# Decode attention with a gated FFN on one core: loading the query weights first, and rearranging the output projection's feeders

## The chip, the core and the metric

The kernel runs on one core of a Trainium2 chip. The metric is the device time in microseconds (us), as the median of several executions. One execution was also recorded by the hardware profiler; its span, 198.8 us, is counted from the first instruction to the last and is a little shorter than the device time of the same execution (200.62 us).

## What is computed

Four decode tokens (B = 4) go through two branches that are mixed by a scalar gate per token. Cut to what matters:

```python
def _A_ref(x, k_cache, v_cache, wq, wo):          # B=4, D=512, Hq=32, Hkv=8, Dh=128
    W = 4096                                      # last 4096 of 16384 cached positions
    q = (x @ wq).reshape(B, 1, 32, 128)           # wq: 512 x 4096
    k = repeat(k_cache[:, :, Sk - W:, :], 4)      # 8 kv heads, each used by 4 query heads
    v = repeat(v_cache[:, :, Sk - W:, :], 4)
    p = softmax(q @ k.T * 128 ** -0.5)
    return (p @ v).reshape(B, 1, 4096) @ wo       # wo: 4096 x 512

def _B_ref(x, W_gate, W_up, W_down):              # 512 x 1792, 512 x 1792, 1792 x 512
    h = relu(x @ W_gate) * (x @ W_up)
    return h @ W_down

g = sigmoid((x * gate_w).sum(-1))
out = g * _A_ref(x, ...) + (1 - g) * _B_ref(x, ...)
```

All of it is bf16 in memory. The keys and values in the window are 4 x 8 x 4096 x 128 elements each, 33.5 MB each. With the weights, 81 MB are read from HBM.

## The kernel before

**Sets.** The attention work is cut into eight sets. Set s is token s % 4 with key-value heads 4*(s // 4) to 4*(s // 4) + 3, so each set reads 4 MB (4096 KB) of keys and 4 MB of values. The 128 partitions of a set hold 4 heads x 32 position blocks of 128 positions.

**Stages of one set.** In the code's names: `KT(s, f)`, four pieces f, turns a quarter of the keys with VectorE's block transpose (`EKT`, L510). `SC(s, f)` multiplies it on TensorE with the query block `qblk` and adds a mask (9 matmuls). `ESC` (L538) copies the scores from PSUM to SBUF and keeps their maxima. After the fourth piece, `MAX`, `SW` and `ESW` (L542 to L550) form one maximum per head. `EXP` (L617) is the softmax's exponential on ScalarE; `PT` (L554) turns the probabilities with a block transpose; `RS` sums the rows; `PV` multiplies the probabilities with the values (32 matmuls); `NORM` (L595) scales the result into `osb`, which has two buffers; `OQ` folds one set's rows of `osb` into the layout that the output projection wants (16 matmuls of 32 columns), and `EOQ` (L602) copies that into `oq`.

**Ends of the kernel.** Before the first set, `XT` turns x, `Z` makes the gate's sum, `Q` multiplies x with wq (32 matmuls), and `EQ`, `QT`, `EQT` spread the queries into `qblk`. After the last scores, `GU` multiplies x with W_gate and W_up (32 matmuls into two PSUM banks, four column groups of the array side by side; the columns of a group are picked with a stride of 14 elements so that the later turn comes out right), `RELU` (L610) and `H` (L562) make the hidden row, `HT` turns it with four TensorE transposes, `EHT` (L568) copies it to SBUF, and `FFN` multiplies it with W_down (28 matmuls) into PSUM bank 7. `T2` (L571) takes that result out of bank 7 and scales it by 1 - g. `WO(p)` then multiplies `oq` with wo in six pieces (64 matmuls) into the same bank 7, `FIN` (L575) adds the two branches, and two small stores write the output.

**Who decides the order.** Everything is written out by hand. `_order()` lists the stages; each engine runs its share of that list in that order, so a stage that waits on TensorE holds every later TensorE stage. `_dma_order()` lists the loads, and all of them are issued by one queue (SP, L247) in that order: a load that has to wait for its buffer holds every load behind it. `_slots()` gives the 4 MB loads four buffers in turn (wg and wu share one), and says what frees each: the fourth `KT` of a set frees its keys, `PV` its values, `Q` the query weights, `GU` the gate and up weights. Waits are put in by name: `WO(p)` waits for its piece of wo, for `T2` (since both results use bank 7) and for every `EOQ`.

The loads of wo in the order of their pieces are 8, 8, 8, 4, 2 and 2 of 32 blocks:

```python
WO_PIECES = ((0, 8), (8, 16), (16, 24), (24, 28), (28, 30), (30, 32))
```

Of the kernel before, what the change touches and what calls it, by code (L numbers as in the profile page):

```python
# [6 lines left out]
BF16 = mybir.dt.bfloat16  # L7
# [9 lines left out]
FF = 1792  # L17
# [78 lines left out]
def _alloc(nc, ctx):  # L96
    R = {}

    def sb(name, shape, dt):
        R[name] = ctx.enter_context(nc.sbuf_tensor(name, shape, dt))  # L100

    sb("slots", [128, NSLOT, 16384], BF16)
    sb("kt", [128, 4, 4096], BF16)
    sb("sc", [128, 2048], BF16)
    sb("pe", [128, 2048], BF16)
    sb("pT", [128, 2, 2048], BF16)
    sb("qblk", [128, NSET, 4, 144], BF16)
    sb("xsb", [4, 512], BF16)
    sb("xT", [128, 16], BF16)
    sb("hT", [128, 56], BF16)  # L110
    sb("gwT", [128, 4], BF16)
    sb("osb", [128, 2, 512], BF16)
# [24 lines left out]


def _order():
    o = [("XT",), ("Z",), ("KT", 0, 0), ("KT", 0, 1), ("KT", 0, 2), ("KT", 0, 3), ("Q",), ("QT",)]  # L140
    o += [("SC", 0, 0), ("SC", 0, 1), ("SC", 0, 2)]
    for s in range(1, NSET):
        o += [("KT", s, 0), ("SC", s - 1, 3)] + [("OQ", s - 2)] * (s > 1) + [("SW", s - 1), ("KT", s, 1), ("PT", s - 1)]
        o += [("SC", s, 0), ("KT", s, 2), ("SC", s, 1), ("RS", s - 1), ("KT", s, 3), ("SC", s, 2), ("PV", s - 1)]
    s = NSET - 1
    o += [("SC", s, 3), ("OQ", s - 1), ("SW", s), ("PT", s), ("RS", s), ("GU",), ("HT",), ("PV", s), ("OQ", s), ("FFN",)]
    return o + [("WO", p) for p in range(len(WO_PIECES))]


def _dma_order():  # L150
    o = [("k", 0), ("x",), ("gw",), ("wq",), ("k", 1), ("v", 0)]
    for s in range(2, NSET):
        o += [("k", s), ("v", s - 1)]
    return o + [("wg",), ("wu",), ("v", NSET - 1), ("wd",)] + [("wo", p) for p in range(len(WO_PIECES))]
# [23 lines left out]
def _program(nc, plan, R, aps):  # L178
# [4 lines left out]
    slots, kt, sc, pe, pT, qblk = R["slots"], R["kt"], R["sc"], R["pe"], R["pT"], R["qblk"]  # L183
    xsb, xT, gwT, osb, oq, hT = R["xsb"], R["xT"], R["gwT"], R["osb"], R["oq"], R["hT"]
    identb, identf, ones = R["identb"], R["identf"], R["ones"]
# [13 lines left out]
    Wo = slot("wo", 0).rearrange("p (i c) -> p i c", i=32)  # L199
    grelu, hrow = sc[:, 0:512], sc[:, 512:1024]  # L200

    trf, scf = {}, {}
    for it in order:
        k = it[0]
        if k == "QT":
            for n in range(2):
                for x in range(2):
                    trf[("QT", n, x)] = len(trf)
        elif k in ("XT", "SW", "RS", "OQ", "HT"):
# [100 lines left out]
    def tensor(t):  # L310
# [41 lines left out]
        def SC(s, f):  # L352
            key = ("SC", s, f)
            bk = banks[scb(key)]
            kv = kt[:, f, :].rearrange("p (t c h k e) -> p t c h k e", t=2, c=16, h=2, k=32)
            w = sc_free(key) + [("QB",), ("ML",), ("MR",), ("E", "KT", s, f)]
            for t in range(2):
# [25 lines left out]

        def OQ(s):
            key = ("OQ", s)
            r = 64 * (s // 4)
            for t in range(2):
                for cc in range(2):
                    for c in range(4):
                        x = 256 * t + 128 * cc + 32 * c  # L390
                        first, lastmm = (t, cc, c) == (0, 0, 0), (t, cc, c) == (1, 1, 3)
                        mm(banks[tr(key)][r:r + 64, 0:32], R["fold"][:, 2 * cc + t, c, :], osb[:, s % 2, x:x + 32], first,
                           lastmm, ev=key if lastmm else None, pos=(0, r),
                           waits=tr_free(key) + [("NORM", s), ("FOLD", 7)] if first else ())

        def gu_n(j):
            return 512 if j < 2 else 384

        def gu_cols(W, q, j):
            g = W[:, FF * q:FF * q + FF].rearrange("p (k i) -> p i k", i=14)  # L400
            return g[:, j:14:4, :]
# [24 lines left out]

        def WO(p):
            lo, hi = WO_PIECES[p]
            w = [("WO", p), ("T2",)] + [("E", "OQ", s) for s in range(NSET)]
            for i in range(lo, hi):  # L430
# [4 lines left out]

        fns = dict(XT=XT, Z=Z, Q=Q, QT=QT, SC=SC, PV=PV, SW=SW, RS=RS, OQ=OQ, WO=WO, GU=GU, HT=HT, FFN=FFN)
        for it in order:
# [4 lines left out]
    for it in order:  # L442
# [10 lines left out]
        elif k == "QT":  # L453
            dve += [("EQT", 0), ("QB",)]
            act += [("EQT", 1)]
# [5 lines left out]
        elif k == "GU":  # L461
            act.append(("RELU",))
            dve.append(("H",))
        elif k == "HT":
            dve.append(("EHT",))
        elif k == "FFN":
# [33 lines left out]
    def vector(v):  # L500
# [28 lines left out]

        def QB():  # L530
            E.op(lambda: v.memset(R["mx4"][:, :], 0.0), ev=("QB",), waits=[("E", "QT", n, 1) for n in range(2)])

        def ESC(s, f):
            key = ("SC", s, f)
            w = [key]
            if f == 0:
                w += [("EXP", s - 1), ("MAX", s - 1)] if s > 0 else [("QT", 1, 1), ("QB",)]
            E.op(lambda: v.tensor_scalar(sc[:, 512 * f:512 * f + 512], banks[scb(key)], 1.0, None, op0=ALU.mult,  # L538
# [22 lines left out]
        def H():  # L561
            E.op(lambda: v.tensor_tensor(hrow, grelu, banks[scb(("GU", 1))], ALU.mult), ev=("H",),  # L562
                 waits=[("RELU",), ("GU", 1)])
            plan.ev[("E", "GU", 1)] = plan.ev[("H",)]

        def EHT():
            ht_src = bankb[tr(("HT",))][:, 0:512].rearrange("p (i x) -> p i x", x=32)[:, 0:14, 0:4]
            E.op(lambda: v.tensor_copy(hT[:, :].rearrange("p (i b) -> p i b", b=4), ht_src), ev=("E", "HT"), waits=[("HT",)])  # L568

# [7 lines left out]

        fns = dict(INIT=INIT, EKT=EKT, EXT=EXT, EQ=EQ, G=G, EQT=EQT, QB=QB, ESC=ESC, MAX=MAX, ESW=ESW, EPT=EPT, ERS=ERS, H=H, EHT=EHT, T2=T2, FIN=FIN)
        for it in dve:
            fns[it[0]](*it[1:])  # L580

    def scalar(a):
# [11 lines left out]
        def NORM(s):  # L594
            E.op(lambda: a.activation(osb[:, s % 2, :], ob(s), ACTF.Copy, scale=recip[:, s % 2:s % 2 + 1]),  # L595
                 ev=("NORM", s), waits=[("E", "RS", s), ("PV", s)] + ([("OQ", s - 2)] if s >= 2 else []))

        def EOQ(s):
            key = ("OQ", s)
            b, qq = set_of(s)  # L600
            r = slice(64 * qq, 64 * qq + 64)
            E.op(lambda: a.activation(oq[r, :, b], banks[tr(key)][r, 0:32], ACTF.Copy), ev=("E",) + key, waits=[key])  # L602

# [5 lines left out]
        def RELU():  # L609
            E.op(lambda: a.activation(grelu, banks[scb(("GU", 0))], ACTF.Relu), ev=("RELU",),  # L610
                 waits=[("GU", 0), ("EXP", NSET - 1)])
# [43 lines left out]
```

## Time and profile before

| | |
|---|---|
| device time, median of 3 | 200.34 us (199.98 to 200.61) |
| span of the profiled execution | 198.8 us |
| TensorE matmul busy | 126.6 us, 64% |
| VectorE busy | 127.0 us, 64% |
| ScalarE busy | 31.8 us, 16% |
| read from HBM | 81.01 MB, 407 GB/s over the span |
| share of the 16 DMA engines taken by the load queue | 95.6% |

The page's second part cuts the span into 40 slices of 4.97 us. Its DMA row gives the busy share of the 16 DMA engines in tenths, its GB/s row what they moved. Where the DMA row stays at 9, compute engines that are busy or idle make no difference to the speed at that point, unless a load is waiting for a buffer that they hold. So three places have to be looked at: the start before the first bytes, any slice in the middle with less than its neighbours, and what is left to do after the last bytes.

### The profile page before, as it was taken

To read this page: it belongs to the slowest core of one execution; us is meant where nothing else is said; L and a number is where in the kernel's file an instruction comes from. 1 tells how busy PE (TensorE), PEld (TensorE's weight loads), DVE (VectorE), ACT (ScalarE), POOL (GpSimd) and SP (SyncE) were. 2 spreads that over 40 slices of the span, in tenths; PEclk is the share of its full clock that TensorE was granted. 3 is DMA by queue.
4 is the path that set the end of the run, shared out by engine and by line. 5 is a ranking of instruction groups with operands and counts; after the bars stand their busy time and mean duration, and the time that the engine had idled before them with its cause. 6 is when DMAs were issued, how large, how long until landed. Compare 5 with 4: busy or idle time off the path is not lost.

```text
span 198.8 us, 2166 instructions
## 1 busy us (share of the span) xinstructions
PE 126.6 (64%) x875; PEld 57.3 (29%) x884; DVE 127.0 (64%) x193; ACT 31.8 (16%) x72; POOL 14.0 (7%) x38
## 2 busy tenths in 40 slices
PE   0010174895579749749875964967595649859875
PEld 0000022342234324324432432422242223311353
DVE  6129564039995997699599499649954994250100
ACT  2000046002201401400140140014001400141010
POOL 7775000000000000000000000000000000000000
PEclk9999995599999999999999999996999997988999
DMA  5999999999999999999999999999999999999970
GB/s 211 422 423 422 437 435 461 442 427 422 422 422 376 422 422 425 442 429 429 438 442 435 422 437 422 425 435 429 429 435 438 420 399 456 441 406 402 421 302 6
DMA packets 3923, 81.16 MB, mean 408 GB/s; under 512 B 572, under 2 KB 584, under 8 KB 968
## 3 DMA queue, kind: packets, MB, share of 16 engines
q1 hardware_dynamic: 3904, 81.01, 95.6%
q8 instruction: 7, 0.11, 0.2%
q14 instruction: 4, 0.03, 0.0%
q10 hardware_dynamic: 8, 0.00, 0.0%
HBM read 81.01 MB, written 0.00 MB: 407 GB/s over the span
## 4 chain that ended last, share of the span: by engine, by line
DVE 35%; DMA 33%; PE 18%; another core or an unknown queue 6%; issue 3%; ACT 2%; SPq 1%; DVEq 0%; ACTq 0%
DMA slots<-in_A_k_cache_dram 22%; DVE kt L510 18%; PE bank L314 17%; DMA slots<-in_A_wq_dram 11%; DVE pT L554 7%; DVE sc L538 5%; DVE qblk L497 2%; PE bank L318 1%; ACT pe L617 1%; ACT qblk L592 1%; SPq L247 1%; DVE rd L544 1%; DVE hmax L549 1%; DVE negmax L550 0%
## 5 line engine op out<-in xcount | busy, mean ns | idle before, releaser
L314 PE MATMUL bank<-kt,qblk 128*128 128x512 bf16 x256 | 66.2, 402 | 25.6 <-DVE kt L510 23.3
L510 DVE STREAM_TRANSPOSE kt<-slots 128x2048 f32<-128x2048 f32 x32 | 73.4, 2300 | 12.1 <-DMA slots<-in_A_k_cache_dram 12.0
L314 PEld LDWEIGHTS bank<-kt,qblk 128*128 128x128 bf16 x256 | 23.5, 100 | 59.8 <-DVE kt L510 27.8
L538 DVE TENSOR_SCALAR_CACHE_REDUCE sc<-bank 128x512 bf16<-128x512 f32 x32 | 21.2, 662 | 19.4 <-remote 13.3
L314 PE MATMUL bank<-slots,pT 128*64 128x512 bf16 x256 | 29.3, 382 | 0.1
L617 ACT ACTIVATE pe<-sc,negmax 128x2048 bf16<-128x2048 bf16 x8 | 16.0, 2002 | 25.7 <-DVE negmax L550 25.7
L554 DVE STREAM_TRANSPOSE pT<-pe 128x2048 bf16<-128x2048 bf16 x8 | 18.5, 2311 | 2.2 <-ACT pe L617 2.2
L595 ACT ACTIVATE osb<-bank,recip 128x512 bf16<-128x512 f32 x8 | 5.5, 687 | 86.7 <-PE bank L314 86.7
L314 PEld LDWEIGHTS bank<-slots,pT 128*64 128x64 bf16 x256 | 13.8, 110 | 15.1 <-issue 3.6
L314 PE MATMUL bank<-slots,xT 128*4 128x512 bf16 (+1 forms) x64 | 10.8, 784 | 9.7 <-DMA slots<-in_A_wq_dram 9.7
L314 PE MATMUL bank<-maskr,maskl 128*128 128x512 bf16 x23 | 9.2, 399 | 0.0
L314 PE MATMUL bank<-rd,grpb 128*128 128x8 bf16 x8 | 1.4, 178 | 12.1 <-DVE rd L544 9.9
L318 PE MATMUL bank<-identb,xsb 4*128 4x4 bf16 x4 | 0.3, 173 | 13.5 <-DMA xsb<-in_A_x_dram 13.5
L314 PEld LDWEIGHTS bank<-slots,xT 128*4 128x4 bf16 x64 | 2.3, 107 | 15.8 <-DMA slots<-in_A_wq_dram 9.8
L314 PE MATMUL bank<-osb,fold 128*64 128x32 bf16 x128 | 5.4, 184 | 1.7 <-ACT osb L595 0.8
L314 PEld LDWEIGHTS bank<-osb,fold 128*64 128x64 bf16 x128 | 4.6, 112 | 4.3 <-issue 3.0
L514 DVE COPY xT<-bank 128x16 bf16<-128x16 bf16 x1 | 0.2, 168 | 8.3 <-PE bank L318 8.3
L571 DVE TENSOR_SCALAR t<-bank,gg 128x256 f32<-128x256 f32 x1 | 0.5, 483 | 6.5 <-PE bank L314 6.5
L314 PEld LDWEIGHTS bank<-rd,grpb 128*128 128x128 bf16 x8 | 0.8, 96 | 13.2 <-DVE rd L544 10.6
L314 PEld LDWEIGHTS bank<-maskr,maskl 128*128 128x128 bf16 x32 | 3.2, 100 | 4.4 <-issue 0.8
L497 DVE COPY qblk<-bank 32x32 bf16<-32x32 bf16 x32 | 4.0, 179 | 0.6 <-PE bank L318 0.5
L562 DVE TENSOR_TENSOR sc<-sc,bank 128x512 bf16<-128x512 bf16 x1 | 0.7, 687 | 5.6 <-remote 5.6
(56 smaller groups left out, 62.4 us busy)
## 6 DMA issues: line engine op xcount, KB each, us to landing
slots<-in_A_k_cache_dram SPq DMA_DIRECT2D x8, 4096.0 KB, 21.3
slots<-in_A_v_cache_dram SPq DMA_DIRECT2D x8, 4096.0 KB, 30.3
slots<-in_A_wq_dram SPq DMA_DIRECT2D x1, 4096.0 KB, 21.5
slots<-in_A_wo_dram SPq DMA_DIRECT2D x3, 1024.0 KB, 19.0
slots<-in_B_W_gate_dram SPq DMA_DIRECT2D x1, 1792.0 KB, 20.1
slots<-in_B_W_up_dram SPq DMA_DIRECT2D x1, 1792.0 KB, 24.0
slots<-in_B_W_down_dram SPq DMA_DIRECT2D x1, 1792.0 KB, 19.0
slots<-in_A_wo_dram SPq DMA_DIRECT2D x1, 512.0 KB, 21.8
```

What stands on the lines that cost most here:

```text
L247: E.op(lambda: e.dma_start(dst, src), ev=ev, waits=waits, ctr=ctr)
L314: E.op(lambda: t.matmul(out_, lhsT, rhs, start=start, stop=stop, tile_position=pos, skip_group_check=True), ev=ev, waits=waits)
L318: E.op(lambda: t.transpose(out_, in_, idn), ev=ev, waits=waits)
L497: E.op(lambda dst=dst, r=r, g=g, e=e, src=src: copy(dst, src[r, g, 0:B, e, :, :]), ev=("E",) + key if (q, g, e) == (3, 1, 1) else None, wa ...
L510: E.op(lambda: v.transpose(kt[:, f, :].bitcast(FP32), slot("k", s)[:, 4096 * f:4096 * f + 4096].bitcast(FP32)), ev=("E", "KT", s, f), waits=w)
L538: E.op(lambda: v.tensor_scalar(sc[:, 512 * f:512 * f + 512], banks[scb(key)], 1.0, None, op0=ALU.mult, op1=ALU.max, accum_out=mx4[:, f:f + ...
L544: E.op(lambda: v.tensor_scalar(rd8[:, :], R["own8"][:, :], rowmax[:, 0:1], None, op0=ALU.mult), ev=("MAX", s), waits=[("RMX", s), ("OWN", ...
L549: E.op(lambda: v.tensor_reduce(hmax[:, :], banks[tr(key)][:, 0:8], AXIS.X, ALU.max), ev=("E",) + key, waits=[key])
L554: E.op(lambda: v.transpose(pT[:, s % 2, :], pe[:, :]), ev=("E", "PT", s), waits=[("EXP", s)] + ([("PV", s - 2)] if s >= 2 else []))
L592: eqt(E, lambda d, x: a.activation(d, x, ACTF.Copy), n)
L595: E.op(lambda: a.activation(osb[:, s % 2, :], ob(s), ACTF.Copy, scale=recip[:, s % 2:s % 2 + 1]), ev=("NORM", s), waits=[("E", "RS", s), ( ...
L617: E.op(lambda: a.activation(pe[:, :], sc[:, :], ACTF.Exp, bias=negmax[:, s % 2:s % 2 + 1], scale=SCALE, accum_out=rowsum[:, s % 2:s % 2 + ...
```

## The change

The change has four parts.

- **Load order.** wq is loaded first, then x and gate_w, then the keys of set 0; before, the keys of set 0 came first. `_order()` follows: `Q` and `QT` come first, and `KT` and `SC` of set 0 are interleaved afterwards. A memset (`QB`, L531) that stood between the spread queries and the first scores is left out, and the first scores wait for the spread queries directly.
- **FFN rows.** The columns of the gate and up weights are read contiguously, 448 for each of the four column groups. The reordering moves into `H`, which reads and writes with strides, and one block transpose on VectorE takes the place of the four TensorE transposes and their copy. The multiply with W_down then takes its left operand from every 32nd group of that result.
- **Fold.** `osb` gets four buffers, and `OQ` folds four sets at once: 16 matmuls of 128 columns twice, in place of 16 matmuls of 32 columns eight times.
- **End.** `PV` of set 6 goes behind `SC` and `SW` of set 7, so that the last scores don't queue behind it on TensorE. `FFN` goes ahead of the last `OQ`.

```diff
 def _order():
-    o = [("XT",), ("Z",), ("KT", 0, 0), ("KT", 0, 1), ("KT", 0, 2), ("KT", 0, 3), ("Q",), ("QT",)]
-    o += [("SC", 0, 0), ("SC", 0, 1), ("SC", 0, 2)]
+    o = [("XT",), ("Z",), ("Q",), ("QT",)] + [("KT", 0, 0), ("KT", 0, 1), ("SC", 0, 0)]
+    o += [("KT", 0, 2), ("SC", 0, 1), ("KT", 0, 3), ("SC", 0, 2)]
     for s in range(1, NSET):
-        o += [("KT", s, 0), ("SC", s - 1, 3)] + [("OQ", s - 2)] * (s > 1) + [("SW", s - 1), ("KT", s, 1), ("PT", s - 1)]
-        o += [("SC", s, 0), ("KT", s, 2), ("SC", s, 1), ("RS", s - 1), ("KT", s, 3), ("SC", s, 2), ("PV", s - 1)]
+        o += [("KT", s, 0), ("SC", s - 1, 3)] + [("OQ", s // 4 - 1)] * (s % 4 == 1 and s > 4) + [("SW", s - 1)]
+        o += [("KT", s, 1), ("PT", s - 1), ("SC", s, 0), ("KT", s, 2), ("SC", s, 1), ("RS", s - 1), ("KT", s, 3)]
+        o += [("SC", s, 2)] + [("PV", s - 1)] * (s < NSET - 1)
     s = NSET - 1
-    o += [("SC", s, 3), ("OQ", s - 1), ("SW", s), ("PT", s), ("RS", s), ("GU",), ("HT",), ("PV", s), ("OQ", s), ("FFN",)]
+    o += [("SC", s, 3), ("SW", s), ("PV", s - 1), ("PT", s), ("RS", s), ("GU",), ("PV", s), ("FFN",), ("OQ", 1)]
     return o + [("WO", p) for p in range(len(WO_PIECES))]

 def _dma_order():
-    o = [("k", 0), ("x",), ("gw",), ("wq",), ("k", 1), ("v", 0)]
+    o = [("wq",), ("x",), ("gw",), ("k", 0), ("k", 1), ("v", 0)]
...
-            w = sc_free(key) + [("QB",), ("ML",), ("MR",), ("E", "KT", s, f)]
+            w = sc_free(key) + [("E", "QT", n, 1) for n in range(2)] + [("ML",), ("MR",), ("E", "KT", s, f)]
...
-        def OQ(s):
+        def OQ(g):
...
-                        mm(banks[tr(key)][r:r + 64, 0:32], R["fold"][:, 2 * cc + t, c, :], osb[:, s % 2, x:x + 32], first,
+                        mm(banks[tr(key)][r:r + 64, 0:128], R["fold"][:, 2 * cc + t, c, :], osb[:, :, x:x + 32], first,
...
-                        mm(banks[scb(fill)][32 * j:32 * j + 4, 0:gu_n(j)], xT[:, 4 * q:4 * q + 4],
-                           gu_cols(W, q, j), q == 0, q == 3,
+                        mm(banks[scb(fill)][32 * j:32 * j + 4, 0:448], xT[:, 4 * q:4 * q + 4],
+                           W[:, FF * q + 448 * j:FF * q + 448 * j + 448], q == 0, q == 3,
...
-        def HT():
-            key = ("HT",)
-            for g in range(4):
-                tp(bankb[tr(key)][:, 128 * g:128 * g + 128], hrow[:, 128 * g:128 * g + 128], identb[:, :],
-                   ev=key if g == 3 else None, waits=tr_free(key) + [("H",), ("IDB",)])
...
-                    mm(banks[ACC][OR * j:OR * j + 4, 0:OW], hT[:, 4 * i:4 * i + 4], Wd[:, x:x + OW], i == 0, i == 13,
+                    mm(banks[ACC][OR * j:OR * j + 4, 0:OW], hT[:, 32 * i:32 * i + 4], Wd[:, x:x + OW], i == 0, i == 13,
...
-            E.op(lambda: v.tensor_tensor(hrow, grelu, banks[scb(("GU", 1))], ALU.mult), ev=("H",),
+            E.op(lambda: v.tensor_tensor(hrow.rearrange("p (i k) -> p i k", i=14), by_i(grelu),
+                                         by_i(banks[scb(("GU", 1))][:, 0:448]), ALU.mult), ev=("H",),
...
-            E.op(lambda: v.tensor_copy(hT[:, :].rearrange("p (i b) -> p i b", b=4), ht_src), ev=("E", "HT"), waits=[("HT",)])
+            E.op(lambda: v.transpose(hT, hrow), ev=("E", "HT"), waits=[("H",)])
...
-            E.op(lambda: a.activation(osb[:, s % 2, :], ob(s), ACTF.Copy, scale=recip[:, s % 2:s % 2 + 1]),
-                 ev=("NORM", s), waits=[("E", "RS", s), ("PV", s)] + ([("OQ", s - 2)] if s >= 2 else []))
+            E.op(lambda: a.activation(osb[:, s % 4, :], ob(s), ACTF.Copy, scale=recip[:, s % 2:s % 2 + 1]),
+                 ev=("NORM", s), waits=[("E", "RS", s), ("PV", s)] + ([("OQ", 0)] if s >= 4 else []))
```

More of the change, by code (lines that the diff above doesn't have):

```diff
@@ L109, in _alloc @@
     sb("xT", [128, 16], BF16)
-    sb("hT", [128, 56], BF16)
     sb("gwT", [128, 4], BF16)
-    sb("osb", [128, 2, 512], BF16)
+    sb("osb", [128, 4, 512], BF16)
     sb("oq", [128, 32, 4], BF16)
@@ L183, in _program @@
     slots, kt, sc, pe, pT, qblk = R["slots"], R["kt"], R["sc"], R["pe"], R["pT"], R["qblk"]
-    xsb, xT, gwT, osb, oq, hT = R["xsb"], R["xT"], R["gwT"], R["osb"], R["oq"], R["hT"]
+    xsb, xT, gwT, osb, oq = R["xsb"], R["xT"], R["gwT"], R["osb"], R["oq"]
     identb, identf, ones = R["identb"], R["identf"], R["ones"]
@@ L199, in _program @@
     Wo = slot("wo", 0).rearrange("p (i c) -> p i c", i=32)
-    grelu, hrow = sc[:, 0:512], sc[:, 512:1024]
+    grelu, hrow, hT = sc[:, 0:448], sc[:, 512:960], sc[:, 1024:1472]
     trf, scf = {}, {}
@@ L208, in _program @@
                     trf[("QT", n, x)] = len(trf)
-        elif k in ("XT", "SW", "RS", "OQ", "HT"):
+        elif k in ("XT", "SW", "RS", "OQ"):
             trf[it] = len(trf)
@@ L382, in PV @@
                        (f, c) in ((3, 12), (3, 14)), ev=("PV", s) if (f, c) == (3, 14) else None, waits=w, pos=(0, r))
-        def OQ(s):
-            key = ("OQ", s)
-            r = 64 * (s // 4)
+        def OQ(g):
+            key = ("OQ", g)
+            r = 64 * g
             for t in range(2):
@@ L391, in OQ @@
                         first, lastmm = (t, cc, c) == (0, 0, 0), (t, cc, c) == (1, 1, 3)
-                        mm(banks[tr(key)][r:r + 64, 0:32], R["fold"][:, 2 * cc + t, c, :], osb[:, s % 2, x:x + 32], first,
+                        mm(banks[tr(key)][r:r + 64, 0:128], R["fold"][:, 2 * cc + t, c, :], osb[:, :, x:x + 32], first,
                            lastmm, ev=key if lastmm else None, pos=(0, r),
[L394 to L401, printed above, removed]
+                           waits=tr_free(key) + [("NORM", 4 * g + 3), ("FOLD", 7)] if first else ())
         def GU():
@@ L428, in WO @@
             lo, hi = WO_PIECES[p]
-            w = [("WO", p), ("T2",)] + [("E", "OQ", s) for s in range(NSET)]
+            w = [("WO", p), ("T2",)] + [("E", "OQ", g) for g in range(2)]
             for i in range(lo, hi):
@@ L434, in WO @@
                        pos=(0, OR * j))
-        fns = dict(XT=XT, Z=Z, Q=Q, QT=QT, SC=SC, PV=PV, SW=SW, RS=RS, OQ=OQ, WO=WO, GU=GU, HT=HT, FFN=FFN)
+        fns = dict(XT=XT, Z=Z, Q=Q, QT=QT, SC=SC, PV=PV, SW=SW, RS=RS, OQ=OQ, WO=WO, GU=GU, FFN=FFN)
         for it in order:
@@ L453, in _program @@
         elif k == "QT":
-            dve += [("EQT", 0), ("QB",)]
+            dve.append(("EQT", 0))
             act += [("EQT", 1)]
@@ L462, in _program @@
             act.append(("RELU",))
-            dve.append(("H",))
-        elif k == "HT":
-            dve.append(("EHT",))
+            dve += [("H",), ("EHT",)]
         elif k == "FFN":
@@ L528, in EQT @@
             eqt(E, v.tensor_copy if v else None, n)
-        def QB():
-            E.op(lambda: v.memset(R["mx4"][:, :], 0.0), ev=("QB",), waits=[("E", "QT", n, 1) for n in range(2)])
         def ESC(s, f):
@@ L536, in ESC @@
             if f == 0:
-                w += [("EXP", s - 1), ("MAX", s - 1)] if s > 0 else [("QT", 1, 1), ("QB",)]
+                w += [("EXP", s - 1), ("MAX", s - 1)] if s > 0 else [("QT", 1, 1)]
             E.op(lambda: v.tensor_scalar(sc[:, 512 * f:512 * f + 512], banks[scb(key)], 1.0, None, op0=ALU.mult,
@@ L561, in H, with by_i @@
         def H():
-            E.op(lambda: v.tensor_tensor(hrow, grelu, banks[scb(("GU", 1))], ALU.mult), ev=("H",),
+            def by_i(t):
+                return t.rearrange("p (k i) -> p i k", i=14)
+            E.op(lambda: v.tensor_tensor(hrow.rearrange("p (i k) -> p i k", i=14), by_i(grelu),
+                                         by_i(banks[scb(("GU", 1))][:, 0:448]), ALU.mult), ev=("H",),
                  waits=[("RELU",), ("GU", 1)])
@@ L566, in EHT @@
         def EHT():
-            ht_src = bankb[tr(("HT",))][:, 0:512].rearrange("p (i x) -> p i x", x=32)[:, 0:14, 0:4]
-            E.op(lambda: v.tensor_copy(hT[:, :].rearrange("p (i b) -> p i b", b=4), ht_src), ev=("E", "HT"), waits=[("HT",)])
+            E.op(lambda: v.transpose(hT, hrow), ev=("E", "HT"), waits=[("H",)])
         def T2():
@@ L576, in FIN @@
                  ev=("OSUM",), waits=[("WOP", len(WO_PIECES) - 1), ("T2",), ("G",)])
-        fns = dict(INIT=INIT, EKT=EKT, EXT=EXT, EQ=EQ, G=G, EQT=EQT, QB=QB, ESC=ESC, MAX=MAX, ESW=ESW, EPT=EPT, ERS=ERS, H=H, EHT=EHT, T2=T2, FIN=FIN)
+        fns = dict(INIT=INIT, EKT=EKT, EXT=EXT, EQ=EQ, G=G, EQT=EQT, ESC=ESC, MAX=MAX, ESW=ESW, EPT=EPT, ERS=ERS, H=H, EHT=EHT, T2=T2, FIN=FIN)
         for it in dve:
@@ L594, in NORM, with EOQ @@
         def NORM(s):
-            E.op(lambda: a.activation(osb[:, s % 2, :], ob(s), ACTF.Copy, scale=recip[:, s % 2:s % 2 + 1]),
-                 ev=("NORM", s), waits=[("E", "RS", s), ("PV", s)] + ([("OQ", s - 2)] if s >= 2 else []))
[L598 to L602, printed above, removed]
+            E.op(lambda: a.activation(osb[:, s % 4, :], ob(s), ACTF.Copy, scale=recip[:, s % 2:s % 2 + 1]),
+                 ev=("NORM", s), waits=[("E", "RS", s), ("PV", s)] + ([("OQ", 0)] if s >= 4 else []))
+        def EOQ(g):
+            key = ("OQ", g)
+            r = slice(64 * g, 64 * g + 64)
+            E.op(lambda: a.activation(oq[r, :, :].rearrange("p i b -> p b i"),
+                                      banks[tr(key)][r, 0:128].rearrange("p (b i) -> p b i", b=4), ACTF.Copy),
+                 ev=("E",) + key, waits=[key])
         def GE():
@@ L609, in RELU @@
         def RELU():
-            E.op(lambda: a.activation(grelu, banks[scb(("GU", 0))], ACTF.Relu), ev=("RELU",),
+            E.op(lambda: a.activation(grelu, banks[scb(("GU", 0))][:, 0:448], ACTF.Relu), ev=("RELU",),
                  waits=[("GU", 0), ("EXP", NSET - 1)])
```

## The prediction

> **What bounds the kernel.** I read the page's slices first.
>
> ```profile
> DMA  5999999999999999999999999999999999999970
> GB/s 211 422 423 422 437 435 461 442 427 422 422 422 376 422 422 425 442 429 429 438 442 435 422 437 422 425 435 429 429 435 438 420 399 456 441 406 402 421 302 6
> ```
>
> The DMA engines are busy from the first slice to the last but one. VectorE and TensorE are busy 64%, so the loads bound the kernel. The low figures are 376 in slice 12 (60 to 65 us) and 302 near the end. I then asked for busy times by stretch (columns: stretch and length, busy time and instructions of PE, PEld, DVE, ACT, POOL, granted clock, DMA share, GB/s).
>
> ```profile
> 3.00:58.00 55.00, 23.66 (x124) 10.21 (x126) 31.91 (x71) 7.86 (x40) 11.88 (x29) 0.91 1.00 430
> 56.00:76.00 20.00, 15.48 (x104) 7.17 (x108) 17.46 (x23) 3.01 (x4) 0.00 (x0) 1.00 1.00 415
> 76.00:186.00 110.00, 80.33 (x523) 34.74 (x527) 77.02 (x102) 18.70 (x25) 0.00 (x0) 0.95 1.00 429
> 186.00:191.50 5.50, 4.66 (x64) 2.80 (x62) 0.00 (x0) 0.92 (x2) 0.00 (x0) 1.00 0.99 408
> 191.50:195.00 3.50, 2.87 (x54) 2.17 (x52) 0.48 (x1) 0.00 (x0) 0.00 (x0) 1.00 0.36 136
> ```
>
> The rate is 430 before and 429 after, but 415 between 56 and 76 us: 20 x (429 - 415) / 429 = 0.65 us lost. The share of 1.00 hides it, since it counts the time of packets and not their bytes. The load queue's timeline has the cause.
>
> ```profile
> 22.82 0.53 SPq L247 DMA_DIRECT2D slots<-in_A_k_cache_dram  x1
> 27.33 0.54 SPq L247 DMA_DIRECT2D slots<-in_A_v_cache_dram  x1
> 58.81 0.54 SPq L247 DMA_DIRECT2D slots<-in_A_k_cache_dram  x1
> ...
> 170.31 2.70 SPq L247 DMA_DIRECT2D slots<-in_A_wo_dram  x6
> ```
>
> The keys of set 3 are issued at 58.81, when the fourth `KT` of set 1 frees a buffer. Six 4 MB loads (25.2 MB) were issued by then; at 430 GB/s from 2.0 us they last until about 61. The queue ran nearly dry and restarted. Later issues come with more in hand: compute needs 16.9 us a set (`negmax` at 48.46, 65.39 and 82.32), the loads 8.39 MB / 429 = 19.6.
>
> The end comes from the issue table of the loads (KB each, us to landing) and from TensorE's timeline.
>
> ```profile
> slots<-in_A_v_cache_dram SPq DMA_DIRECT2D x1, 4096.0 KB, 31.2
> slots<-in_B_W_down_dram SPq DMA_DIRECT2D x1, 1792.0 KB, 19.0
> slots<-in_A_wo_dram SPq DMA_DIRECT2D x2, 256.0 KB, 22.1
> ```
>
> ```profile
> 176.65 7.51 PE L314 MATMUL bank<-slots,xT 128*4 128x512 bf16 x32
> 185.03 0.40 PE L318 MATMUL bank<-identb,sc 128*128 128x128 bf16 x4 [0.88 <-DVE sc L562]
> 185.36 3.64 PE L314 MATMUL bank<-slots,pT 128*64 128x512 bf16 x32
> 189.85 0.68 PE L314 MATMUL bank<-osb,fold 128*64 128x32 bf16 x16 [0.84 <-ACT osb L595]
> 190.46 1.69 PE L314 MATMUL bank<-slots,hT 128*4 128x256 bf16 x28
> 192.78 3.66 PE L314 MATMUL bank<-slots,oq 128*4 128x256 bf16 x64 [0.63 <-issue]
> ```
>
> The last values were issued at 149.26 and land at 149.26 + 31.2 = 180.5; W_down 165.79 + 19.0 = 184.8; the last wo piece 172.6 + 22.1 = 194.7. So `PV` of set 7 starts 4.9 us after its data: `GU` (7.51 us) is ahead of it. `WO` starts at 192.78, runs its 64 matmuls without a pause, and ends at 196.44, 1.7 us after the last bytes. Then `FIN` takes 0.48 and the stores 1.84 to 198.8.
>
> [...]the chain shows 8 matmuls of scores in 3.59 us at 35.42 and 1.91 at 55.96. [...]`GU`, with a stride of 28 bytes, takes 7.51 us where `Q`, contiguous, took 3.29 for the same count.
>
> **The change, part by part.**
>
> *Load order.* wq lands at about 13.4 (where the keys of set 0 did), the keys at about 24.0 (where wq did): same bytes, same start. `Q` to `EQT` took from 23.99 to 35.2, 11.2 us; from 13.9 (x still lands at 13.5) they end near 25.2, mostly while the keys arrive. Then at 24.0 the transposes begin. Two (2.30 each) end at 28.6; `SC(0,0)` starts near 26.3, and at half clock takes 4 us, so `ESC(0,0)` ends at 31.0; `KT`, `ESC`, `KT`, `ESC` (2.3 + 0.66 twice) end at 36.9, where `KT(1,0)` begins. It began at 44.60 before: 7.7 us earlier. The keys of set 3 are issued at about 51, ten before the queue is dry. The 0.65 us are recovered. The removed memset (0.06 us) lies in the hidden part.
>
> *Fold in the middle.* Six of eight `OQ` go, 0.68 us each on TensorE and 0.24 on ScalarE; `OQ(0)` grows to 128 columns. From `PV`, 512 columns take 3.64/32 = 0.114 us with two column groups side by side, thus 0.23 for one; 128 columns cost 0.057, and 16 cost 0.9 us. TensorE is 64% busy and waits for keys; worth nothing. The new wait (set 4's `NORM` for `OQ(0)`) has `OQ(0)` issued before `PV` of set 4, so it is met.
>
> *FFN rows.* `GU` goes from 7.51 to Q's 3.29 us (6.6 at half clock). `H` keeps its 0.69 for 448 instead of 512 columns; bounds for the strides are 0.6 and 1.4. The block transpose replaces 0.40 + 0.19: 2048 columns took 2.31, so 448 take 0.51. The sum saves some 4 us on TensorE ahead of `PV`.
>
> *End.* `SC(7,3)` no longer waits for `PV(6)` (3.64 us); the chain of scores to probabilities ends near 174.6 instead of 178.6. `PV(6)` now ends near 173.5, and the wo loads, which wait for its buffer, are issued 3.2 us later, with v and W_down in hand until 184.8: hidden. `GU` then runs 173.7 to 177.0, `H` and the transpose to 178.3. On the times of before, `PV(7)` starts with its data at 180.5, ends at 184.1; `FFN` (1.69) starts at 184.8, ends at 186.5; `OQ(1)` 187.5, `EOQ` near 187.9. `WO` has 60 of its 64 matmuls, 60 x 0.057 = 3.4 us, to do before the last piece at 194.7, and meets each piece as it lands. Slack: 194.7 - 187.9 - 3.4 = 3.4 us. Half clock in `PV(7)` would add up to 3.6[...].
>
> *Sum.* Last bytes 194.7 - 0.65 = 194.05; the last piece's 4 matmuls 0.23 to 0.46, waits 0.1, `FIN` 0.48, stores 1.84: 196.8 at 0.3. The span shortens by 2.0 to 2.1; 200.34 - 2.1 = 198.2.
>
> **Rivals.**
>
> *The recovered stretch is lost elsewhere* (0.17). [...] Then only the tail counts: 196.44 to 194.7 + 0.3 is 1.4 us, giving 198.9. For it: the uneven finish in the last stretch.[...]
>
> *The engines finish more evenly* (0.12). Some 200 fewer TensorE instructions need fewer fetches[...]: 197.3. The trace doesn't say whether the slowest engine gains.
>
> *TensorE still ends after the loads* (0.05). With half clock in `GU`, `PV(7)` and `OQ`, `WO` ends as late as before: 200.3. Against it: 3.4 us of slack.
>
> *The first sets are later, not earlier* (0.06; slower). The four transposes of set 0 (8.9 us), which lay under wq's load, now come after the keys. If they don't overlap with the scores and `KT(1,0)` starts at 47 instead of 44.6, the queue runs dry for 2.4 us more; less the tail's 1.4, that is +1.0: 201.3. Against it: what used to follow wq's landing was longer (11.2 us), and it is hidden now.
>
> **How the numbers follow.** My forecast has 0.60, and the rivals 0.17, 0.12, 0.05 and 0.06. The time is 198.2. From 197.0 to 199.5 the range takes in the second rival, the first, and 0.3 us either way of spread between executions; the last two, and a little of each tail, are left out. Faster by over 0.3% (under 199.74): 0.60 + 0.17 + 0.12, less a little, 0.88. Within 0.3%: 0.06. Slower: 0.06.
>
> **What would show it.** Right: keys of set 3 issued near 51; no stretch under 425 GB/s between 20 and 185; last bytes near 194; `GU` near 3.3 us; `PV(7)` starting as its values land; `WO` in pieces with idle time before them that a load ends, the last one of 4 matmuls. Wrong: `WO` in one block as before (TensorE late), or a low stretch in a new place (a buffer freed late), or last bytes at 194.7 or after.

## The result, and the profile after

The changed kernel takes 197.61 us (median of 4, 197.38 to 198.00), the kernel before 200.16 beside it. The ratio is 0.9882, 95% interval 0.9838 to 0.9926: 2.4 us faster. Run again with the experiments it was 197.91 (197.60 to 198.26), ratio 0.9894 (0.9848 to 0.9941). The forecast of 198.2, 2.1 us faster, holds, though 197.61 lies nearer to the 197.3 of the rival in which the engines finish more evenly. Medians and ranges, here and below, count all executions; ratios leave out those that took over 1.5% longer than the fastest of their kernel.

The page's slices after:

```profile
DMA  6999999999999999999999999999999999999990
GB/s 220 441 415 428 456 448 441 418 429 428 434 441 434 434 424 434 428 428 428 428 428 428 424 428 428 441 423 441 418 448 428 434 409 440 429 409 419 420 386 30
```

The 376 of slice 12 is gone; that slice now has 434. Single slices of 5 us still scatter from 409 to 456. By my estimate a slice holds only some 65 packets of 32 KB (7 packets moved 0.23 MB between 172.4 and 173 in the kernel before), so I compare longer stretches: 36 to 76 us of the kernel before, then 36 to 76 us and 76 to 186 us after (columns as in the prediction: GB/s last).

```profile
36.00:76.00 40.00, 29.58 (x160) 12.84 (x162) 30.47 (x41) 5.11 (x6) 0.00 (x0) 0.94 0.99 420
```

```profile
36.00:76.00 40.00, 25.88 (x150) 10.99 (x147) 31.87 (x41) 5.57 (x6) 0.00 (x0) 1.00 1.00 430
76.00:186.00 110.00, 78.82 (x466) 34.73 (x466) 74.06 (x96) 17.68 (x20) 0.00 (x0) 0.89 1.00 428
```

The first stretch rises from 420 to 430; the second, 429 before, stays. The load queue's timeline after shows why:

```profile
0.80 0.39 SPq L247 DMA_DIRECT2D slots<-in_A_wq_dram  x1
...
50.07 0.54 SPq L247 DMA_DIRECT2D slots<-in_A_k_cache_dram  x1
```

The keys of set 3 are issued at 50.07 instead of 58.81. Further down, VectorE's first transpose of set 7 waits for its keys, which makes a good clock of the loads. Before, and after:

```profile
151.61 2.31 DVE L510 STREAM_TRANSPOSE kt<-slots 128x2048 f32<-128x2048 f32 x1 [4.67 <-DMA slots<-in_A_k_cache_dram]
```

```profile
150.41 2.31 DVE L495 STREAM_TRANSPOSE kt<-slots 128x2048 f32<-128x2048 f32 x1 [4.67 <-DMA slots<-in_A_k_cache_dram]
```

The keys land 1.2 us sooner. The end of TensorE's timeline after:

```profile
172.74 1.69 PE L314 MATMUL bank<-slots,xT 128*4 128x448 bf16 x32
179.24 5.33 PE L314 MATMUL bank<-slots,pT 128*64 128x512 bf16 x32 [4.81 <-DMA slots<-in_A_v_cache_dram]
184.50 1.69 PE L314 MATMUL bank<-slots,sc 128*4 128x256 bf16 x28
186.12 1.08 PE L314 MATMUL bank<-osb,fold 128*64 128x128 bf16 x16
187.83 1.91 PE L314 MATMUL bank<-slots,oq 128*4 128x256 bf16 x32 [0.63 <-ACT oq L586]
190.90 1.04 PE L314 MATMUL bank<-slots,oq 128*4 128x256 bf16 x16 [1.16 <-DMA slots<-in_A_wo_dram]
192.14 1.02 PE L314 MATMUL bank<-slots,oq 128*4 128x256 bf16 x12 [0.20 <-DMA slots<-in_A_wo_dram]
193.42 0.38 PE L314 MATMUL bank<-slots,oq 128*4 128x256 bf16 x4 [0.26 <-DMA slots<-in_A_wo_dram]
```

`PV` of set 7 now waits 4.81 us for its values, where it used to be late for them. The final multiply is split by idle time that the wo loads end, and its last four matmuls start when the last piece lands, near 193.4. The chain of work that ended last says the same (start, length, what):

```profile
175.60 17.77 DMA slots<-in_A_wo_dram
193.42 0.40 PE bank L314 x4
```

So of the 2.6 us between the two spans (198.8 and 196.2), 1.3 come from the last bytes (194.7 to 193.4) and 1.3 from the matmuls behind them (1.7 us to 0.4).

### The profile page after: what moved, and what is told of

Read it like the earlier page. It is cut to its first block, busy times and chain, and to the rows that moved or that the text cites. A ratio compares the mean times of both kernels' runs of the same rounds, so it can differ in the third digit from the quotient of the medians.

```text
span 196.2 us, 1966 instructions
## 1 busy us (share of the span) xinstructions
PE 125.9 (64%) x784; PEld 56.3 (29%) x784; DVE 127.7 (65%) x192; ACT 30.7 (16%) x66; POOL 14.1 (7%) x38
## 4 chain that ended last, share of the span: by engine, by line
DMA 56%; DVE 32%; PE 7%; SPq 2%; issue 1%
DMA slots<-in_A_k_cache_dram 47%; DVE kt L495 21%; DMA slots<-in_A_wo_dram 9%; PE bank L314 7%; DVE sc L520 5%; DVE pT L536 5%; SPq L247 2%; DVE rd L526 1%; DVE rowmax L524 0%; DVE hmax L531 0%; DVE negmax L532 0%; DVE osum L560 0%; DVE recip L541 0%
## 5 line engine op out<-in xcount | busy, mean ns | idle before, releaser
L314 PE MATMUL bank<-kt,qblk 128*128 128x512 bf16 x256 | 70.8, 423 | 21.7 <-DVE kt L495 21.7
L314 PEld LDWEIGHTS bank<-kt,qblk 128*128 128x128 bf16 x256 | 24.7, 104 | 59.6 <-DVE kt L495 26.1
L314 PE MATMUL bank<-slots,pT 128*64 128x512 bf16 x256 | 30.8, 396 | 4.8 <-DMA slots<-in_A_v_cache_dram 4.8
L314 PEld LDWEIGHTS bank<-slots,pT 128*64 128x64 bf16 x256 | 14.9, 114 | 19.9 <-issue 9.3
L314 PE MATMUL bank<-maskr,maskl 128*128 128x512 bf16 x32 | 13.0, 408 | 0.0
L314 PE MATMUL bank<-slots,oq 128*4 128x256 bf16 x64 | 4.3, 272 | 2.3 <-DMA slots<-in_A_wo_dram 1.6
L314 PE MATMUL bank<-slots,xT 128*4 128x512 bf16 (+1 forms) x64 | 5.3, 489 | 0.0
L560 DVE SCALAR_TENSOR_TENSOR osum<-bank,gg,t 128x256 bf16<-128x256 f32 x1 | 0.5, 484 | 7.1 <-PE bank L314 7.1
L577 ACT ACTIVATE qblk<-bank 32x32 bf16<-32x32 bf16 x32 | 3.5, 179 | 2.7 <-PE bank L318 2.6
```

The source lines that it names most:

```text
L314: E.op(lambda: t.matmul(out_, lhsT, rhs, start=start, stop=stop, tile_position=pos, skip_group_check=True), ev=ev, waits=waits)
L577: eqt(E, lambda d, x: a.activation(d, x, ACTF.Copy), n)
```

## The experiments

All times are medians; ratios are to executions of the kernel before that ran beside them, with 95% intervals. The span and the timeline of a run are those of one recorded execution.

### The load order alone

```diff
-    o = [("k", 0), ("x",), ("gw",), ("wq",), ("k", 1), ("v", 0)]
+    o = [("wq",), ("x",), ("gw",), ("k", 0), ("k", 1), ("v", 0)]
```

with the first two lines of `_order()` as in the change; all else as before.

> The kernel before with the new load order and the matching order of the first stages, and nothing else. Theory (two gains of the loads: the first load starts its bytes about 0.5 us sooner, and the restart near 60 us, about 0.65 us, goes away; the work after the last scores hangs on the landing of the keys of set 7, so it moves with them): keys of set 3 issued near 50, keys of set 7 landing near 150.4 instead of 151.6, the final block of 64 matmuls still in one piece, the span 1.2 us shorter, 197.6. Rival (the recovered stretch is lost elsewhere[...]): keys of set 7 land at 151.6 or later, no gain. Rival (the end is TensorE's alone and not tied to the loads): keys earlier, but the block still ends at 196.4, no gain.

Measured: 198.36 us, ratio 0.9937 (0.9909 to 0.9965). The clock of the loads and the final multiply in its trace:

```profile
150.53 2.31 DVE L510 STREAM_TRANSPOSE kt<-slots 128x2048 f32<-128x2048 f32 x1 [4.68 <-DMA slots<-in_A_k_cache_dram]
```

```profile
190.08 3.97 PE L314 MATMUL bank<-slots,oq 128*4 128x256 bf16 x64 [0.63 <-issue]
```

The keys of set 3 are issued at 52.30, those of set 7 land at 150.53, and the block reads as one piece. The ratio is 1.3 us of 200, as expected. The expected issue near 50 and span of 197.6 were off; the span is 196.4. In this recording the third scores of set 7 took 1.91 us where the recording of before had 3.20 (8 matmuls each; the granted clock was 1.00 here and 0.57 before). The chain that ended last shows what that did:

```profile
169.87 23.75 DMA slots<-in_A_wo_dram
...
193.66 0.40 PE bank L314 x4
```

The last four matmuls start as the last piece lands, at 193.6: in this recording TensorE is no longer late, although the block has no gap long enough to split its line. So how late TensorE is under the old end differs between executions by more than a microsecond, single spans mix that with the loads, and I rely on the ratios.

### The end alone

The changed kernel with the old first two lines of `_order()`, and:

```diff
-    o = [("wq",), ("x",), ("gw",), ("k", 0), ("k", 1), ("v", 0)]
+    o = [("k", 0), ("x",), ("gw",), ("wq",), ("k", 1), ("v", 0)]
```

> The changed kernel with the old load order and the old order of the first stages: FFN rows, fold and end changed. Theory: the last bytes land near 194.7 as before, the final multiply follows the pieces and ends 0.4 us after the last one, the span is 197.5, 1.4 us shorter than before and 1.3 longer than the changed kernel. Rival (the engines finish more evenly with fewer instructions): the last bytes land at 194.2 or before and the span is 197.0 or less. Rival (the load order gave nothing, all of the gain is the tail): 196.2 as the changed kernel.

Measured: 198.32 us (198.01 to 198.61), ratio 0.9893 (0.9848 to 0.9938), span 196.8. The keys of set 7 land at 151.68, as before; the last four matmuls start at 194.00, when their piece lands. The tail follows the loads as expected. The last piece came 0.7 us sooner than before, though, and the span is below 197.0, so by its numbers the second case, more even engines because of fewer instructions, is met. Other traces speak against its reason. From the landing of the keys of set 7 to that of the last piece, this run took 42.3 us and the kernel before 43.1; but the moves alone, below, which drop no matmul, took 42.4, and the changed kernel, with as few instructions as this run, 43.0. The finish differs by that much between recordings, whatever the number of instructions. With 6 executions the interval of the ratio reaches from 1.2 to 3.0 us of gain. This ratio and that of the load order add up to 1.7%, more than the whole change's 1.2%, and both intervals allow the smaller sum.

### The FFN rows alone

The kernel before with the new `GU`, `RELU`, `H`, `EHT` and `FFN` of the change, no `HT`, and no other edit; cut to two lines:

```diff
-                           gu_cols(W, q, j), q == 0, q == 3,
+                           W[:, FF * q + 448 * j:FF * q + 448 * j + 448], q == 0, q == 3,
...
-            E.op(lambda: v.tensor_copy(hT[:, :].rearrange("p (i b) -> p i b", b=4), ht_src), ev=("E", "HT"), waits=[("HT",)])
+            E.op(lambda: v.transpose(hT, hrow), ev=("E", "HT"), waits=[("H",)])
```

> The kernel before with the FFN rows alone changed: contiguous gate and up columns, strided H, block transpose instead of four TensorE transposes; old load order, old fold, old order of the stages at the end. Theory (either part of the tail's change is enough, because both open more room than the 1.4 us that separate TensorE from the loads): gate and up end near 179 instead of 184, PV of set 7 starts as its values land near 180.5, the final multiply follows the pieces of wo, span 197.5. Rival (the moves are what counts): PV of set 7 starts no earlier than 184, span 198.5 or more.

```profile
175.90 3.01 PE L313 MATMUL bank<-slots,xT 128*4 128x448 bf16 x32
```

```profile
180.61 3.65 PE L313 MATMUL bank<-slots,pT 128*64 128x512 bf16 x32 [1.70 <-DMA slots<-in_A_v_cache_dram]
```

Measured: 198.71 us, ratio 0.9942 (0.9917 to 0.9966). `GU` falls from 7.51 to 3.01 us, `PV` starts as its values land, and the last four matmuls start with their piece at 194.76: 0.06 us later than the 194.7 of before. So this part alone removes TensorE from the end of this recording; the ratio is worth 1.2 us. The recorded execution, 199.25 us, is one of the slower of its 22 (197.94 to 200.19), and it ends with its loads, whose last piece lands 0.8 us later than in the run of the end alone.

### The moves alone

```diff
-    o += [("SC", s, 3), ("OQ", s - 1), ("SW", s), ("PT", s), ("RS", s), ("GU",), ("HT",), ("PV", s), ("OQ", s), ("FFN",)]
+    o += [("SC", s, 3), ("SW", s), ("PV", s - 1), ("PT", s), ("RS", s), ("GU",), ("HT",), ("OQ", s - 1), ("PV", s), ("FFN",), ("OQ", s)]
```

and no `PV(6)` in the loop above it; strided reads and TensorE transposes stay.

> The kernel before with the moves at the end alone: PV of set 6 behind the scores and the maxima of set 7, FFN ahead of the last fold, the fold of set 6 just ahead of PV of set 7; strided gate and up reads, TensorE transposes and load order as before. Theory (either part is enough): the last probabilities are ready near 174.6 instead of 178.6, gate and up end near 181.5, PV of set 7 runs from about 182.7 to 186.3, the final multiply starts near 190 and follows the pieces of wo, span 197.5 to 197.9. Rival (the contiguous reads are what counts): the final multiply is still one block that ends after 195.5, span 198.3 or more.

```profile
172.90 7.52 PE L315 MATMUL bank<-slots,xT 128*4 128x512 bf16 x32
```

```profile
193.70 0.38 PE L315 MATMUL bank<-slots,oq 128*4 128x256 bf16 x4 [0.25 <-DMA slots<-in_A_wo_dram]
```

Measured: 198.36 us, ratio 0.9946 (0.9914 to 0.9977), span 196.5. `GU` is as slow as ever, and still the end follows the loads. The span is a microsecond below the expected 197.5 to 197.9; this recording shows no low stretch near 60 us, although the keys of set 3 are issued at 58.60 as before:

```profile
36.00:76.00 40.00, 30.17 (x149) 12.46 (x150) 29.15 (x40) 5.11 (x6) 0.00 (x0) 0.88 1.01 433
```

In the recordings either part is enough: each opens several microseconds of room in front of a gap of 1.7. The medians agree that the gains don't add, 198.71 and 198.36 for the parts and 198.32 for the end as a whole. The ratios don't settle it: 1.2 and 1.1 us for the parts, 1.2 to 3.0 for the whole.

### The fold alone

The kernel before with the new `OQ`, `EOQ` and `NORM`, the places of `OQ` that follow from them, and no other edit:

```diff
-    sb("osb", [128, 2, 512], BF16)
+    sb("osb", [128, 4, 512], BF16)
...
-        o += [("KT", s, 0), ("SC", s - 1, 3)] + [("OQ", s - 2)] * (s > 1) + [("SW", s - 1), ("KT", s, 1), ("PT", s - 1)]
+        o += [("KT", s, 0), ("SC", s - 1, 3)] + [("OQ", s // 4 - 1)] * (s % 4 == 1 and s > 4) + [("SW", s - 1), ("KT", s, 1), ("PT", s - 1)]
```

> The kernel before with the fold of four sets alone: load order, FFN rows and the other stages of the end as before. Theory (the folds that go lie where TensorE waits, the one at the end grows from 0.68 to about 1.1 us on the path): 0 to 0.4 us slower than before, ratio 1.000 to 1.002. Rival (fewer TensorE instructions mean one instruction fetch less and a more even end of the loads): 0.3 us or more faster, ratio 0.998 or less.

```profile
188.64 1.08 PE L314 MATMUL bank<-osb,fold 128*64 128x128 bf16 x16 [0.84 <-ACT osb L595]
```

Measured: 200.51 us, ratio 1.0026 (0.9998 to 1.0054). The six folds that went are worth nothing, and the one at the end costs 1.08 us instead of 0.68 where TensorE is on the path. The expected loss of up to 0.4 us fits; the interval just includes no change. In the changed kernel the fold lies in the slack.

### The late issue put back, in three steps

In the changed kernel, what frees the buffer for the keys of set 3:

```diff
-        frees[n] = {"k": [("E", "KT", it[-1], 3)], ...
+        frees[n] = {"k": [("SC", 2, 0)] if it == ("k", 1) else [("E", "KT", it[-1], 3)], ...
```

The other two runs have `("E", "PT", 1)` and `("E", "KT", 2, 0)` in place of `("SC", 2, 0)`.

The changed kernel ran again beside the first two of these.

> The changed kernel as it is, run beside the next three on one chip. Expected 197.6, 0.987 to 0.988 of the kernel before, with all executions within 0.7 us of each other, since its end hangs on the loads and not on TensorE's clock.

> The changed kernel, with the keys of set 3 issued after the first scores of set 2 (near 58.9) instead of near 50: as long before the queue is empty as in the kernel before, all else as changed. Theory (an issue so late makes the queue restart, and that is paid at the end in full): a stretch of less than 425 GB/s between 56 and 76 us, the last bytes 0.5 to 0.9 us later, 198.3. Rival (only an empty queue costs, and 2 us of slack are enough): 197.6, no low stretch.

> The same with the keys of set 3 issued after the probabilities of set 1 are turned (near 61.7), when the queue has just run empty. Theory: at the start of the program the first 32 KB packets ended 3.3 us after their issue, so here they end near 65.0 instead of 62.3 to 64: 1.5 to 2.7 us lost and paid at the end, 199.7. Rival (the loads catch up, because the keys wait for VectorE anyway): under 198.5.

> The changed kernel with the keys of set 3 issued after the first transpose of set 2 (near 55.6): 5.5 us before the queue would be empty, between the changed kernel (near 50) and the late issue (59.4). Theory (a late issue costs only when the queue is within some 3 us of empty): as the changed kernel, 197.6 to 197.9, executions within 0.7 us of each other, no low stretch. Rival (each microsecond of issue counts): between the two, 198.5 or more, wide spread.

| keys of set 3 issued at | time, range | ratio (95%) | keys of set 7 land |
|---|---|---|---|
| 50.51 (changed kernel) | 197.91 (197.60 to 198.26) | 0.9894 (0.9848 to 0.9941) | 150.74 |
| 56.16 | 197.98 (197.91 to 198.08) | 0.9893 (0.9860 to 0.9925) | 150.95 |
| 59.43 | 199.37 (197.53 to 201.10) | 0.9974 (0.9946 to 1.0003) | 152.00 |
| 63.34 | 201.72 (200.09 to 203.15) | 1.0065 (1.0038 to 1.0092) | 154.94 |

The stretch from 36 to 76 us, for 56.16, 59.43 and 63.34 in turn:

```profile
36.00:76.00 40.00, 28.34 (x148) 11.76 (x149) 31.98 (x40) 5.56 (x6) 0.00 (x0) 0.91 1.00 430
```

```profile
36.00:76.00 40.00, 26.09 (x151) 11.09 (x148) 30.51 (x39) 5.57 (x6) 0.00 (x0) 1.00 0.99 424
```

```profile
36.00:76.00 40.00, 27.91 (x151) 11.54 (x149) 29.20 (x38) 5.57 (x6) 0.00 (x0) 0.96 0.91 389
```

The stretch falls with the issue, the keys of set 7 land later with it, and the time follows. The changed kernel itself came out 0.3 us above the expected 197.6. An issue at 56.16 is free. At 59.43, by the forecast's estimate 1.6 us before the queue is empty, the median loses 1.5 us, twice what I expected (1.6 by the ratios; 1.2 if the four slowest of the 22 executions are left out, and even then the rest differ by 2.9 us). At 63.34 the loss is 3.8 us; I had expected an issue at 61.7 and 1.5 to 2.7, and 1.6 us of the difference are the later issue. In that recording the DMA share from 56 to 76 us is 0.83, at 350 GB/s: its engines were idle for an estimated 0.17 of 20, 3.4 us. At the start of the program, the first load is issued at 0.80 and the first packets start at 1.8 in the changed kernel and 2.2 in the kernel before, 1.0 and 1.4 us later. With the same delay after 63.34 the queue ran empty near 61, and an issue at 59.43 has a few tenths in hand at most, not 2 us; both are estimates from these numbers. The case that the loads catch up is refuted. This one late issue takes back more than half of what the whole change gained.

### Tiny loads first

In the changed kernel:

```diff
-    o = [("wq",), ("x",), ("gw",), ("k", 0), ("k", 1), ("v", 0)]
+    o = [("x",), ("gw",), ("wq",), ("k", 0), ("k", 1), ("v", 0)]
```

> The changed kernel with x and gate_w, which are tiny, issued ahead of wq: the first 4 MB load is issued near 1.5 instead of 0.8. Theory (a kernel whose loads never pause pays the start of the first large load in full): the last bytes 0.5 to 0.7 us later, 198.2 to 198.5. Rival (the start is hidden, because the end hangs on something else): 197.6 to 197.9.

Measured: 198.34 us (198.10 to 198.64), ratio 0.9911 (0.9879 to 0.9942), against 197.98 and 0.9893 for the kernel with the issue at 56.16, run beside it. wq is issued at 1.64 instead of 0.80, 0.84 us later; the keys of set 7 land at 151.08, 0.1 to 0.7 later than in the six recordings with wq first and the keys of set 3 issued by 57. The loss of 0.4 us is a little under the expected 0.5 to 0.7. The trace and the median agree that the start is paid, at about half of its 0.84 us, but the intervals overlap.

### Does TensorE's clock make the spread under the old end?

The load order alone, plus ten matmuls without use into bank 7 between the row sums of set 6 and the third scores of set 7:

```diff
+        def WARM():
+            for _ in range(10):
+                mm(banks[ACC], identb[:, :], R["maskr"][:, :], True, True, waits=[("GE",), ("IDB",), ("MR",)])
```

> The kernel before with the load order alone (as the run of that edit), plus ten matmuls without use into bank 7 that fill TensorE's idle time between the row sums of set 6 and the third scores of set 7. Theory (with the old end TensorE is on the path, and executions differ by whether those scores fall into a half-clock stretch, 3.2 us instead of 1.9): the slower group of executions (199.5 to 200.1 without the ten) goes, the median falls to 198.1. Rival (the groups come from the loads, a late engine): both groups stay, median 198.4 or more.

Measured: 198.27 us (197.81 to 200.38), ratio 0.9936 (0.9912 to 0.9960), against 0.9937 for the load order alone. In its recording the scores took 1.92 us, as in the recording without the ten matmuls (1.91), so the two traces don't tell the cases apart. Of 22 executions 3 took 199.5 us or more, of the 19 without the ten matmuls 7 did; but the median and the ratio did not move. What makes the executions of these kernels differ stays open: the traces show two candidates, the third scores (1.91 or 3.20 us) and late loads (the last piece of wo from 193.7 to 194.8 under the old order).

### Load order and FFN rows, without the moves and the fold

The edits of the first and the third experiment together, on the kernel before:

```diff
-    o = [("k", 0), ("x",), ("gw",), ("wq",), ("k", 1), ("v", 0)]
+    o = [("wq",), ("x",), ("gw",), ("k", 0), ("k", 1), ("v", 0)]
...
-                           gu_cols(W, q, j), q == 0, q == 3,
+                           W[:, FF * q + 448 * j:FF * q + 448 * j + 448], q == 0, q == 3,
```

> The kernel before with the load order and the FFN rows, but the old fold (one set at a time) and the old places of PV of set 6 and of FFN. Theory (what counts is the load order, and room on TensorE at the end, which the FFN rows alone give): as the changed kernel, ratio 0.987 to 0.990, executions within 0.8 us of each other. Rival (the moves or the fold are needed as well): ratio 0.992 or more, a group of executions 1 us or more above the rest.

Measured: 198.04 us (197.55 to 198.84), ratio 0.9920 (0.9891 to 0.9949), span 195.8. The keys land at 150.77 and the last matmuls start with their piece at 193.06. The ratio lies on the border that I had drawn, and its interval holds both the changed kernel's ratio and the rival's. Its executions differ by 1.3 us, more than the 0.8 expected. The trace is on the side of the theory: no TensorE work is left behind the loads; and the median is 0.1 us above those of the changed kernel (197.91) and of the issue at 56.16 (197.98). A difference of up to half a percent between this and the full change isn't excluded.

## Why the prediction was right

**The loads bound the kernel**: shown. Only edits that let the loads start or run on sooner, or that shorten what comes behind them, moved the time. Six folds of 0.68 us each went from a TensorE that was 64% busy and gave nothing (ratio 1.0026). From 36 to 76 and from 76 to 186 us no recording moved more than 433 GB/s; that loads in mid-stream can't go faster was not shown.

**The recovered stretch**: the mechanism was right. The issue near 51 came at 50.07, `KT(1,0)` near 36.9 at 35.89, and an issue at 59.43 took more than half of the gain back. That issue is 0.6 us later than the one of before, so its 1.5 us are not what the kernel before lost. The term of 0.65 us was read from one recording, and the low stretch is not in every recording of the old order: with an issue between 58.4 and 58.7, the stretch from 36 to 76 us moved 433 GB/s in the moves alone, 432 in the fold alone, 428 in the end alone and 423 in the FFN rows alone, against 430 to 433 in all seven with the new order and no late issue. On the average of the recordings (next paragraph) some 0.6 to 0.8 us are left for it, near the forecast; in the pair that I compared, the last bytes came 1.3 us sooner, not 0.65. The gain was larger than forecast, 2.4 or 2.6 instead of 2.1.

**"Same bytes, same start"**: wrong, in a term that the forecast put at nothing. The queue spent 0.39 us issuing wq as first load, 0.63 on the keys, and the first bytes moved earlier. Kernel before, then after (a packet counts where it starts, hence the 590):

```profile
1.50:2.00 0.50, 0.00 (x0) 0.00 (x0) 0.50 (x1) 0.50 (x1) 0.43 (x2) 1.00 0.00 0
```

```profile
1.50:2.00 0.50, 0.00 (x0) 0.00 (x0) 0.50 (x1) 0.50 (x1) 0.43 (x2) 1.00 2.32 590
```

In six recordings with wq first and no late issue the keys of set 7 land at 150.4 to 151.0, in five with the old order at 151.3 to 152.5. The load order is thus worth about 1 us in the loads on average, of which the start is an estimated 0.2 to 0.4: the first packets start 0.4 us later in the kernel before (2.2) than in the changed one (1.8), and with the tiny loads first wq is issued 0.84 us later, which lost 0.4.

**The tail**: right in its sum, 1.7 us behind the last bytes turned into 0.4. Its terms were off in both directions and cancelled. `GU` took 1.69 us, not 3.29: I had priced it by `Q`, which starts after 9.69 us of idle time and took 0.103 us a matmul where `GU` took 0.053. That this was the price of half the clock is my estimate; the traces don't show it for `Q`. What they show of the clock: in the kernel before, the 8 matmuls of scores that took 3.59 us at 35.42 were granted 0.50 of it, those that took 1.91 at 55.96 all of it (1.00); with the FFN rows alone `GU` starts shortly after 2.57 us of idle time and took 3.01 us, and the granted clock from 175 to 180 was 0.66. `H` with its strides took 0.95 us (bounds 0.6 to 1.4), the block transpose 0.65 instead of 0.51, the last fold 1.08 instead of 0.9. `PV(7)` started with its data after a wait of 4.81 us and took 5.33 us instead of 3.64: TensorE was granted 0.73 of its clock between 180 and 185. The longer time used 1.7 of the 3.4 us of slack. With the end alone it was much the same, 5.13 us at 0.72 after a wait of 4.85. `WO` started at 187.83, forecast 187.9; since `PV(7)` started 1.3 us sooner and took 1.7 us longer than in the forecast, this agreement is luck. The 1.7 us behind the last bytes are themselves those of one recording, with the third scores at 0.57 of the clock; with the load order alone they were 0.4 under the same old end. That the forecast came within 0.3 us of the measured gain is therefore in part luck.

**The later wo issue**: hidden, as forecast. It moved from 170.31 to 172.54, and no gap follows: the 5.5 us from 184.8 on moved 409 GB/s, those from 186 in the kernel before 408.

**The rivals.** TensorE did not end after the loads, the first sets did not get later, and the recovered stretch was not lost elsewhere. A more even finish because of fewer instructions is not supported: the instruction queue (q8 on the page) moved 6 packets after and 7 before, and the recordings' finishes differ by up to 0.8 us, but not along with the number of instructions (42.3 and 43.0 us after the keys of set 7 with fewer, 42.4 and 43.1 with all). What makes them differ stays open.

**A test that I set too sharply**: "no stretch under 425 GB/s between 20 and 185" fails on single slices (409, 418) of an undisturbed queue. Stretches of 40 us do tell 420 from 430: those of the undisturbed recordings lie within 3 GB/s.

## What to carry to other kernels

In a kernel bound by its loads, look for the last moment at which each load may be issued, not only for an idle DMA queue: here, with the queue empty near 61 by estimate, an issue 5 us before that (56.16) cost nothing, and one some 2 us before (59.43) cost about 1.5 us and made the time uneven, while the busy share still read 0.99. One recording doesn't tell what such a late issue costs: with issues 0.2 us apart one showed 420 GB/s and another 433. Then look at what stands between the last bytes and the last instruction, and stop when it follows the loads: in these recordings either of two edits opened enough room. Small loads at the very start were paid in part at the end: 0.4 of 0.84 us.

## What was not expected of the hardware

- A load that is issued before the queue is empty can still cost time: at 59.43, by estimate some 2 us ahead, the median rose by 1.5 us and 22 executions ranged over 3.6 us; at 56.16 six ranged over 0.2. From the issue of the very first load to its first packets 1.0 us passed in the changed kernel and 1.4 in the kernel before.
- Reading the gate and up weights on TensorE with a stride of 28 bytes made 32 matmuls take 7.52 us in the moves alone; contiguous reads of as many columns took 1.69 in the changed kernel: over four times as long, both at a granted clock of 1.00.
- The issue of the first load took 0.39 us for a weight matrix with one long row per partition and 0.63 for the keys, for the same 4 MB. The layout alone doesn't set that time: as fourth load of the kernel before, wq took 0.69.
